# Exchanging the PSUM homes of two kinds of sums, and making weight differences earlier

## The chip, the cores and the metric

The program runs on one core of a Trainium2 chip. The metric is the device time of one execution in microseconds, the median of three runs. A profiled execution gives the trace that is read below.

## The reference

Three layers follow one another. All data are float32.

```
attention   batch 4, heads 8, sequence 576, head dimension 64
  scores = q k^T / 8 + cum[i] - cum[j],  cum = cumsum(log(clip(f, 1e-4, 1)));  causal;  softmax;  times v
  the output is laid out as x: 2304 tokens x 512
first MLP   h = x @ w_in (512 x 1024);  solu = h * softmax(h);  layer norm * g_ln;  @ w_out (1024 x 512)
second MLP  h = max(x @ w2_in (512 x 2048), 0);  out = (h * h) @ w2_out (2048 x 512)
```

## The kernel before

**Order of the work.** All work is entered as steps into a planner (class Plan, line 28). A step has the engines that it may run on with an estimated time on each, the keys that it reads and writes, a priority, and perhaps a slot that it takes from a ring (pp: three one-bank PSUM tiles, hp: two slots, rq: eleven SBUF places for squared products). `lay` puts the steps in an order by these estimates, and the program is emitted in that order. Every engine then works off its own instructions in order. The waits between engines are put in from the tiles that instructions touch, not from the planner's keys. All DMAs are issued from SP's queue, in order.

**PSUM.** Eight banks: `Z` is two tiles of one bank each (z0, z1), `XO` one bank, `HP` (line 325) one tile of two banks, `PP` three tiles of one bank each. In attention z0 and z1 hold scores, XO the sums over v, HP the 1024 products of the first MLP of one token block.

**Precision.** A float32 matmul is three: each operand is split in a high and a low part (`halves`, line 1082: a copy that rounds and a subtraction), and low by high, high by low and high by high are added up in PSUM.

**Second MLP.** It is computed by seven products in place of eight. Hidden columns go in 8 pairs (p = 0 to 7, 256 columns each), tokens in 9 blocks of 256. Block 0 goes through `half_up` (line 1270): 24 matmuls per p into one PSUM bank, then relu and square on ACT. Blocks 1 and 2, 3 and 4, ... go through `unit(b, p)` (line 1300): seven products of six matmuls each in two banks. Products 0 and 1 share the first bank, 2 and 3 the second; they are read (one copy on ACT, three adds on DVE), and products 4, 5 and 6 are added on top of 0, 2 and 3, and read again. Units with odd number take their two banks from ring pp, units with even number take both slots of HP. `half_up` uses pp for p = 0 and 1 and a slot of HP from p = 2 on (HPP).

`step(blk, p)` (line 1376) forms differences of the squared products on DVE, splits them, and adds 21 matmuls to seven down sums of 256 columns each. Sums 0 and 1 lie in z0, 2 and 3 in z1, 4 and 5 in XO, 6 in a pp slot. PE does the group of sums 0, 3, 1 first and then 5, 6, 2, 4. After p = 7 `fold` (line 1435) reads them all: a copy of sum 0 on ACT, then seven adds on DVE in the order 1, 5, 6, 4, 4, 3, 2. The next block starts its sums in the same banks. The last block uses two slots of HP and two of pp.

Units are numbered n = 8 (b - 1) + p. For each unit two steps are due, so PE goes on as unit 0, steps 0 and 1, unit 1, steps 2 and 3, and so on, with steps laid between the products of a unit.

**Weights of the second MLP.** The inputs come as float64 words. Beside attention, `early2` (line 1023) turns them into float32 by integer operations (`convert`, line 668, ending in an add on POOL at line 703) in five staging places (tile free). w2_out (32 pieces of 128 x 256) is stored as it is to the DRAM tensor w2d. Then w2_in follows: per pair seven combinations for `unit` are made (`add2`, line 1056, may run on DVE or POOL), split (`part2`, line 1044) and stored as high and low parts to w2u; the plain halves for `half_up` go to w2d.

In the second MLP `weights2` (line 1133) loads the two w2_out rows of a pair (two loads of 256 KB into two of six staging slots, `load2`, line 1100), makes four differences on DVE in place (`diff`, line 1149, issued at line 1151), and splits the results a (256 columns), b, s and t (512 each) into their places for `step`. `weightsh` (line 1114) does the loading and splitting for `half_up`; `unit` loads its parts from w2u directly.

Of the kernel before, what the change touches and what calls it, by code (L numbers as in the profile page):

```python
# [240 lines left out]
def tile_kernel(ctx: ExitStack, tc: tile.TileContext, q, k, v, f, w_in, w_out, g_ln, w2_in, w2_out, out):  # L241
# [31 lines left out]

    w2d = dram.tile([KF2, 2, P, 512], F32, name="w2d")
    w2u = dram.tile([KF2 // 2, 7, P, 512], F32, name="w2u")
    sb = ctx.enter_context(tc.tile_pool(name="sb", bufs=1))
    ps = ctx.enter_context(tc.tile_pool(name="ps", bufs=1, space=PSUM))
# [50 lines left out]
    NU, NRQ = 13, 11  # L328
    pl = Plan(dict(pp=3, hp=2, rq=NRQ), ("z0", "z1", "xo", "h"))
    uid = [0]  # L330
# [337 lines left out]
    def convert(src, raw, w, hi, lo, n, prio, rawk, wk, outk, gain=None, to=None):  # L668
# [303 lines left out]
    def rk2(ri):  # L972
        return [("2r", ri, z) for z in range(2)]
# [49 lines left out]
    def early2():  # L1023
# [12 lines left out]
        def unit(n, fc, c, hf, prio):  # L1036
            i = n % 5
            convert(
                source2(fc, 2 * c + hf), lambda: both(i), lambda: place(i, 2), None, None, 256,
                prio, ("fr", i), ("fw", i), ("w2d", fc, c, hf), to=w2d[fc, c, :, hf * 256 : hf * 256 + 256],  # L1040
            )
            return i

        def part2(i, p, k, prio):
# [9 lines left out]
            pl.add(dict(dma=1140), lambda: nc.sync.dma_start(w2u[p, k], both(i)), prio, [lk, hk], [("w2u", p, k)])  # L1054

        def add2(i, x, y, op, prio):
# [4 lines left out]
            s = pl.add(dict(dve=335, pool=686), fn, prio, [("fw", x), ("fw", y)], [("fw", i)], port=True)  # L1061

        n = 0
        for fc in range(KF2):
            for hf in range(2):
                unit(n, fc, 1, hf, EARLY0 + n * EARLYP)
                n += 1
        for p in range(KP):
            prio = EARLY1 + p * EARLYQ
            a11, a12, a21, a22 = (unit(n + 2 * a + hf, 2 * p + a, 0, hf, prio + EARLYR * (2 * a + hf)) for a in range(2) for hf in range(2))  # L1070
            n += 4
            prio += 4 * EARLYR
            for i, k in ((a11, 0), (a12, 4), (a22, 5)):
                part2(i, p, k, prio)
            add2(a22, a22, a21, ALU.add, prio)
            add2(a21, a11, a21, ALU.subtract, prio)
            add2(a11, a22, a11, ALU.subtract, prio)
            add2(a12, a12, a11, ALU.subtract, prio)
            for i, k in ((a21, 2), (a22, 3), (a11, 1), (a12, 6)):
                part2(i, p, k, prio)  # L1080

# [17 lines left out]

    def load2(fc, c, prio):  # L1100
        ri = turn[0] % len(RAW)
        turn[0] += 1
        once(("raw", ri), RAW[ri], rk2(ri), prio)
        pl.add(
            dict(dma=1140), lambda: nc.sync.dma_start(RAW[ri][0](), w2d[fc, c]), prio - AHEAD,
            [("w2d", fc, c, z) for z in (0, 1)], rk2(ri),
        )
        return ri
# [5 lines left out]
    def weightsh(p, prio):  # L1114
        for c in range(2):
            ri = load2(2 * p + c, 0, prio)
            for a in "hl":
# [15 lines left out]
    def weights2(p, prio):  # L1133
        W = W2[p]
        rr = [load2(2 * p + i, 1, prio) for i in range(2)]

        def place(nm, n):
# [4 lines left out]
        def split(nm, raw, rk, n):  # L1142
            halves(raw, rk, W[nm + "h"][0], ("w2", p, nm + "h"), W[nm + "l"][0], ("w2", p, nm + "l"), n, prio)

        a, b = slice(0, 256), slice(256, 512)
        r = [[lambda i=i, z=z: RAW[rr[i]][0]()[:, z] for z in (a, b)] for i in range(2)]
        k = [rk2(rr[0]), rk2(rr[1])]

        def diff(dst, x, y, rk, wk):
            def fn():  # L1150
                nc.vector.tensor_tensor(out=dst(), in0=x(), in1=y(), op=ALU.subtract)

            pl.add(dict(dve=335), fn, prio, rk, wk, port=True)

        place("a", 256)
        place("b", 512)
        place("s", 512)
        place("t", 512)
# [65 lines left out]
    m7 = ("pp", "m7")  # L1224
    last8 = [("hp", "l0"), ("hp", "l1"), ("pp", "l2"), ("pp", "l3")]

    def bank(blk, i):
        if blk == NTB - 1:
            return last8[(i + 1) // 2 if i == 6 else i // 2]
        return m7 if i == 6 else ("z0", "z1", "xo")[i // 2]  # L1230

    def psum(k):
        if k[0] == "hp":
            return HP[:, pl.slot[k]]
        if k[0] == "pp":
            return at(k)
        return Z[0] if k == "z0" else Z[1] if k == "z1" else XO.rearrange("p c x -> p (c x)")

# [31 lines left out]
    def half_up(p, prio):  # L1270
        uid[0] += 1
        ck = ("pp" if p < HPP else "hp", uid[0])
        if p == HPP:
            pl.add(dict(dve=0), lambda: None, prio - 5000, [], ["h", "hp"])
        W = H2[p]
        for y, c in ((0, 0), (0, 1), (1, 0), (1, 1)):
            def up(y=y, c=c):
# [10 lines left out]

            rk = [("w2", p, f"u{c}{a}") for a in "hl"] + [("xo", 5 + y, a) for a in range(2)] + ["hp"] * (p >= HPP)
            pl.add(  # L1290
                dict(pe=6 * 116), up, prio, rk, [ck] + ["turn"] * (y + c == 0), take=None if y + c else ck,
                uses=[ck] if y + c else [],
            )
        r = new_r(0, p, prio)
        relu(lambda: psum(ck), lambda: psum(ck), 512, prio, [], [ck], [ck], True)
        square(rof(0, p), lambda: psum(ck), 512, prio, [ck, "rqs"], [r], [ck], True, take=r)

    uprods = [(0, 0), (0, 1), (1, 0), (1, 1), (0, 0), (1, 0), (1, 1)]

    def unit(b, p, prio):  # L1300
        n = (b - 1) * KP + p
        pool = "pp" if n % 2 else "hp"
        uid[0] += 2
        ks = [(pool, uid[0] - 1), (pool, uid[0])]
        lastks[pool] = ks
        s1, s2 = (2 * b - 1, p), (2 * b, p)
# [11 lines left out]
        def prod(i, prio):  # L1318
            m = (7 * n + i) % NU
            sk = ("us", m)  # L1320
            if sk not in first_use:
                once(sk, again(upper[m]), [sk], prio)
            pl.add(
                dict(dma=1140), lambda: nc.sync.dma_start(upper[m][0]().bitcast(F32), w2u[p, i]), prio - UAHEAD,
                [("w2u", p, i)], [sk],
            )

            def fn():
# [12 lines left out]
            pl.add(  # L1341
                dict(pe=6 * 116), fn, prio, [sk, ("xo", i, 0), ("xo", i, 1), "hp"], [k] + ["turn"] * (i == 0),
                take=k if opens_ else None, uses=[] if opens_ else [k],
            )

        def add(dst, x, i, prio, rk, wk, uses=(), take=None):
# [3 lines left out]
            k = ks[uprods[i][0]]  # L1350
            pl.add(dict(dve=344), fn, prio, [k] + rk, wk, uses=[k] + list(uses), take=take)

        for i in range(4):
            prod(i, prio)
        copy(TB, u2f, lambda: half(0), prio, [ks[0]], [uk], [ks[0]])
        add(u2f, u2f, 1, prio, [], [uk])
# [5 lines left out]
        for i in (4, 5, 6):  # L1362
# [3 lines left out]
            dict(act=264), lambda: nc.scalar.activation(out=c11(), in_=half(0), func=AF.Relu), prio, [k, "rqs"], [r1],  # L1366
            uses=[k], take=r1,
        )
# [7 lines left out]
    def step(blk, p, prio):  # L1376
# [329 lines left out]
```

## Time and profile before

| | |
|---|---|
| runs | 863.93, 864.44, 867.23 us, median 864.44 |
| profiled execution | 866.17 us, span of its trace 864.4 us |
| PE busy | 805.0 us (93%) |
| DVE busy | 646.6 us (75%) |
| ACT busy | 543.2 us (63%) |
| POOL busy | 369.8 us (43%) |
| data moved | 151.52 MB, mean 175 GB/s |
| mean granted TensorE clock | 0.984 of 2.4 GHz |

Busy time says how long an engine had something running. Attention and the first MLP fill the first 450 us or so; from about 458 us on PE works on the second MLP. The figures are means over stages that differ, so what a change in one stage is worth has to be read from that stage.

### The profile page before, as it was taken

To read this page: it belongs to the slowest core of one execution; us is meant where nothing else is said; L and a number is where in the kernel's file an instruction comes from. 1 tells how busy PE (TensorE), PEld (TensorE's weight loads), DVE (VectorE), ACT (ScalarE), POOL (GpSimd) and SP (SyncE) were. 2 spreads that over 40 slices of the span, in tenths; PEclk is the share of its full clock that TensorE was granted. 3 is DMA by queue.
4 is the path that set the end of the run, shared out by engine and by line. 5 is a ranking of instruction groups with operands and counts; after the bars stand their busy time and mean duration, and the time that the engine had idled before them with its cause. 6 is when DMAs were issued, how large, how long until landed. Compare 5 with 4: busy or idle time off the path is not lost.

```text
span 864.4 us, 18663 instructions
## 1 busy us (share of the span) xinstructions
PE 805.0 (93%) x6392; PEld 729.0 (84%) x6392; DVE 646.6 (75%) x1655; ACT 543.2 (63%) x1383; POOL 369.8 (43%) x528
## 2 busy tenths in 40 slices
PE   4878899999999999999999888999999999999997
PEld 2556687888888888888989788999999999999997
DVE  8797867887767766866658769888678767876777
ACT  6899977988687887887857555454324433533332
POOL 6468767665587767687753010010111121112110
PEclk9999889999999999999999999999999999999999
DMA  6643336655555555645556666484757676665501
GB/s 208 191 146 116 115 94 205 199 175 171 166 165 177 177 154 167 208 160 166 177 191 205 190 205 243 154 279 144 241 178 237 188 229 205 198 207 172 158 1 49
DMA packets 99869, 151.52 MB, mean 175 GB/s; under 512 B 12128, under 2 KB 41824, under 8 KB 99776
## 3 DMA queue, kind: packets, MB, share of 16 engines
q1 hardware_dynamic: 99776, 150.35, 55.0%
q8 instruction: 50, 0.82, 0.4%
q14 instruction: 43, 0.35, 0.1%
HBM read 117.58 MB, written 32.65 MB: 174 GB/s over the span
## 4 chain that ended last, share of the span: by engine, by line
PE 73%; ACT 11%; DVE 11%; issue 3%; POOL 1%; DVEq 0%; ACTq 0%; POOLq 0%
PE hp L1334 9%; PE pp L1334 9%; PE pp L590 5%; PE z L536 5%; PE xo L610 4%; PE z L1420 3%; PE z L1421 3%; PE pp L777 3%; PE z L1422 3%; PE hp L826 3%; PE pp L779 3%; PE pp L778 3%; ACT adj L571 3%; PE hp L828 3%; PE hp L827 3%
## 5 line engine op out<-in xcount | busy, mean ns | idle before, releaser
L536 PE MATMUL z<-k,q 80*64 80x288 f32 (+17 forms) x384 | 95.8, 348 | 11.9 <-DVE q L501 8.2
L571 ACT ACTIVATE adj<-z,st 64x288 f32<-64x288 f32 (+9 forms) x192 | 95.3, 499 | 17.2 <-DVE st L557 15.2
L590 PE MATMUL pp<-ident,adj 128*128 128x128 f32 (+1 forms) x480 | 82.4, 282 | 16.9 <-ACT adj L571 15.2
L590 PEld LDWEIGHTS pp<-ident,adj 128*128 128x128 f32 (+1 forms) x480 | 52.8, 145 | 43.3 <-ACT adj L571 28.5
L557 DVE CUSTOM_DVE_ANT_0 z<-z,maskb 128x128 f32<-128x128 f32 (+8 forms) x144 | 65.4, 464 | 29.6 <-PE z L536 25.7
L777 PE MATMUL pp<-ln,woh 128*128 128x256 f32 x288 | 84.8, 294 | 2.2 <-DVE ln L906 1.5
L345 ACT COPY pt<-pp 128x256 f32<-128x256 f32 (+5 forms) x167 | 68.1, 418 | 24.3 <-PE pp L590 23.2
L779 PE MATMUL pp<-ln,woh 128*128 128x256 f32 x288 | 81.7, 284 | 0.0
L778 PE MATMUL pp<-ln,wol 128*128 128x256 f32 x288 | 81.7, 284 | 0.0
L1087 DVE TENSOR_TENSOR k<-adj,k 128x512 fp32r<-128x512 f32 x75 | 52.4, 700 | 38.2 <-POOL k L349 26.3
L349 POOL TENSOR_SCALAR k<-adj 128x512 fp32r<-128x512 f32 x39 | 24.2, 620 | 124.2 <-DVE adj L1392 50.7
L536 PEld LDWEIGHTS z<-k,q 128*128 128x128 f32 (+3 forms) x384 | 58.7, 189 | 20.0 <-ACT pt L1526 8.2
L703 POOL TENSOR_TENSOR free<-free 128x256 uint32<-128x256 uint32 x64 | 50.8, 799 | 47.5 <-DVE free L697 42.8
L610 PE MATMUL xo<-pt,vn 128*64 128x128 f32 (+1 forms) x960 | 64.9, 277 | 0.4 <-ACT pt L345 0.3
L826 PE MATMUL hp<-wih,xl 128*128 128x512 f32 x144 | 62.6, 435 | 1.1 <-ACT hp L865 1.1
L349 POOL TENSOR_SCALAR ln<-q 128x384 fp32r<-128x384 f32 x29 | 15.5, 534 | 111.6 <-PE z L1422 42.5
L610 PEld LDWEIGHTS xo<-pt,vn 128*64 128x64 f32 x960 | 51.5, 143 | 11.6 <-issue 6.8
L777 PEld LDWEIGHTS pp<-ln,woh 128*128 128x128 f32 x288 | 55.5, 193 | 4.8 <-DVE ln L906 2.0
L827 PE MATMUL hp<-wil,xh 128*128 128x512 f32 x144 | 57.5, 399 | 0.2 <-DVE wil L707 0.2
L828 PE MATMUL hp<-wih,xh 128*128 128x512 f32 x144 | 57.4, 399 | 0.0
L778 PEld LDWEIGHTS pp<-ln,wol 128*128 128x128 f32 x288 | 55.9, 194 | 0.6
L779 PEld LDWEIGHTS pp<-ln,woh 128*128 128x128 f32 x288 | 55.9, 194 | 0.0
(594 smaller groups left out, 2619.3 us busy)
## 6 DMA issues: line engine op xcount, KB each, us to landing
ln<-w2u SPq DMA_DIRECT2D x119, 256.0 KB
k<-w2u SPq DMA_DIRECT2D x105, 256.0 KB
w2u<-free SPq DMA_DIRECT2D x56, 256.0 KB
kn<-in_k_dram SPq DMA_DIRECT2D x32, 256.0 KB
free<-in_moe_w_out_dram SPq DMA_DIRECT2D x32, 256.0 KB
w2d<-free SPq DMA_DIRECT2D x64, 128.0 KB
free<-in_moe_w_in_dram SPq DMA_DIRECT2D x32, 256.0 KB
vn<-in_v_dram SPq DMA_DIRECT2D x20, 256.0 KB
```

Of the source, the lines that this page charges most:

```text
L345: nc.scalar.copy(dst(), src())
L536: nc.tensor.matmul(dst, lhsT=ql[0:r, p, 0:m], rhs=rhs, start=(g == 0), stop=(g == 1))
L571: nc.scalar.activation(out=adj[0:m, c[1] : c[2]], in_=Z[c[0]][0:m, 0 : c[2] - c[1]], func=AF.Exp, bias=st[0:m, low : low + 1], scale=-1.0, ...
L590: nc.tensor.transpose(at(sk)[:, (c - g) * m : (c - g + 1) * m], adj[0:m, zc : zc + P], ident[0:m, 0:m])
L610: nc.tensor.matmul(XO[own[j], g // 2, off : off + m], lhsT=VN[vslot[b, c]][:, (g + j) * D : (g + j + 1) * D], rhs=PT[(s - h + g + j) % NPT ...
L777: nc.tensor.matmul(px, lhsT=woh[:, fc, w], rhs=lo, start=(fc == 0), stop=False)
L778: nc.tensor.matmul(px, lhsT=wol[:, fc, w], rhs=hi, start=False, stop=False)
L779: nc.tensor.matmul(px, lhsT=woh[:, fc, w], rhs=hi, start=False, stop=(fc == KF - 1))
L826: nc.tensor.matmul(HP[:, c], lhsT=XL[i][:, cc, :], rhs=wih[:, cc, w], start=(cc == 0), stop=False)
L827: nc.tensor.matmul(HP[:, c], lhsT=XH[i][:, cc, :], rhs=wil[:, cc, w], start=False, stop=False)
L828: nc.tensor.matmul(HP[:, c], lhsT=XH[i][:, cc, :], rhs=wih[:, cc, w], start=False, stop=(cc == KC - 1))
L1334: nc.tensor.matmul(half(i), lhsT=l, rhs=r[:, x], start=(i in (0, 2) and c + k == 0), stop=(c + k == 3), skip_group_check=True,)
```

## The change

The two kinds of sums exchange homes. Units with an even number and all of `half_up` use z0 and z1; down sums 0 to 3 use the two banks of HP (keys h0 and h1). The last block's sums 0 to 3 use z0 and z1 in place of HP.

The differences of w2_out are made in `early2`, beside attention, with `add2`. For pairs 0 to 6 the seven pieces of 128 x 256 (a, b in two, s in two, t in two) are stored as float32 to w2f, and `weights2` loads them in four loads and splits them. For the last pair (NPRE = 1) the pieces are split in `early2` as well and stored to w2s, and `weights2` loads high and low parts straight into their places, in eight loads. The planner's estimate of such loads goes from 1140 to 900 ns per 256 KB (LOAD2).

```diff
-    w2d = dram.tile([KF2, 2, P, 512], F32, name="w2d")
+    w2d = dram.tile([KF2, P, 512], F32, name="w2d")
+    w2f = dram.tile([KF2 // 2 - NPRE, 7, P, 256], F32, name="w2f")
+    w2s = dram.tile([NPRE, 7, P, 512], F32, name="w2s")
...
-    more("k10", 5, 1, upper)
+    upper += carve("k10", [512] * 5)
...
+        def keep(i, p, k, prio):
+            if p >= KP - NPRE:
+                part2(i, w2s[p + NPRE - KP, k], ("w2s", p, k), prio)
+            else:
+                pl.add(dict(dma=570), lambda: nc.sync.dma_start(w2f[p, k], place(i, 2)), prio, [("fw", i)], [("w2f", p, k)])
...
-        for fc in range(KF2):
-            for hf in range(2):
-                unit(n, fc, 1, hf, EARLY0 + n * EARLYP)
-                n += 1
+        for p in range(KP):
+            prio = EARLY0 + 4 * p * EARLYP
+            r00, r01, r10, r11 = (
+                unit(n + 2 * a + hf, 2 * p + a, 1, hf, prio + EARLYP * (2 * a + hf)) for a in range(2) for hf in range(2)
+            )
+            n += 4
+            prio += 4 * EARLYP
+            for i, k in ((r00, 0), (r10, 1), (r11, 2)):
+                keep(i, p, k, prio)
+            add2(r00, r01, r00, ALU.subtract, prio)
+            add2(r01, r11, r01, ALU.subtract, prio)
+            for i, k in ((r00, 3), (r01, 4)):
+                keep(i, p, k, prio)
+            add2(r11, r11, r00, ALU.subtract, prio)
+            add2(r10, r11, r10, ALU.subtract, prio)
+            for i, k in ((r10, 5), (r11, 6)):
+                keep(i, p, k, prio)
...
     def weights2(p, prio):
-        rr = [load2(2 * p + i, 1, prio) for i in range(2)]
-        split("a", r[0][0], k[0][0:1], 256)
-        diff(r[0][0], r[0][1], r[0][0], k[0][1:], k[0][0:1])
-        split("b", RAW[rr[1]][0], k[1], 512)
-        diff(r[0][1], r[1][1], r[0][1], k[1][1:], k[0][1:])
-        split("s", RAW[rr[0]][0], k[0], 512)
-        diff(r[1][1], r[1][1], r[0][0], k[0][0:1], k[1][1:])
-        diff(r[1][0], r[1][1], r[1][0], k[1][1:], k[1][0:1])
-        split("t", RAW[rr[1]][0], k[1], 512)
+        for nm, n in (("a", 256), ("b", 512), ("s", 512), ("t", 512)):
+            if p < KP - NPRE:
+                src = w2f[p, c[0]] if n == 256 else w2f[p, c[0] : c[0] + 2].rearrange("c p x -> p c x")
+                ri = load2(src, [("w2f", p, k) for k in c], n, prio)
...
+                continue
+            for y, a in enumerate("hl"):
+                def fn(dst=W[nm + a][0], c=c, n=n, y=y):
+                    src = w2s[p + NPRE - KP, c[0] : c[0] + n // 256, :, y * 256 : y * 256 + 256]
...
-    last8 = [("hp", "l0"), ("hp", "l1"), ("pp", "l2"), ("pp", "l3")]
+    last8 = ["z0", "z1", ("pp", "l2"), ("pp", "l3")]
-        return m7 if i == 6 else ("z0", "z1", "xo")[i // 2]
+        return m7 if i == 6 else ("h0", "h1", "xo")[i // 2]
...
     def half_up(p, prio):
-        ck = ("pp" if p < HPP else "hp", uid[0])
+        ck = f"z{p % 2}"
...
     def unit(b, p, prio):
-        pool = "pp" if n % 2 else "hp"
-        ks = [(pool, uid[0] - 1), (pool, uid[0])]
+        ks = [("pp", uid[0] - 1), ("pp", uid[0])] if n % 2 else ["z0", "z1"]
...
-HPP = 2
+NPRE, LOAD2 = 1, 900
```

## Rows read from the trace of the kernel before

**Rows 1.** The page: the chain that ended last, shares by engine.

```profile
PE 73%; ACT 11%; DVE 11%; issue 3%; POOL 1%; DVEq 0%; ACTq 0%; POOLq 0%
```

**Rows 2.** What PE waited for, 458 to 845 us: total, times, longest (us).

```profile
PE hp L1334 <- DVE xw L1348: 3.5, 4, 1.0
PE hp L1334 <- ACT xw L345: 3.2, 6, 0.9
PE hp L1334 <- ACT q L1366: 3.2, 6, 0.7
PE hp L1284 <- ACT q L1253: 2.2, 3, 0.7
PE hp L1284 <- ACT hp L1248: 2.2, 3, 0.8
PE hp L1334 <- issue: 1.5, 1, 1.5
PE hp L1334 <- ACT adj L1366: 0.9, 2, 0.5
PE hp L1334 <- ACT xh L1366: 0.9, 2, 0.5
PE z L1420 <- DVE ln L1087: 0.6, 1, 0.6
PE hp L1334 <- ACT qn L1366: 0.5, 1, 0.5
PE hp L1284 <- ACT adj L1253: 0.4, 1, 0.4
```

**Rows 3.** Timeline of PE: start, us, engine, line, operation, [idle before <-releaser].

```profile
616.55 0.87 PE L1334 MATMUL pp<-woh,ln 128*128 128x256 f32 x6
...
626.44 0.87 PE L1334 MATMUL hp<-woh,ln 128*128 128x256 f32 x6
627.15 1.57 PE L1334 MATMUL hp<-wol,ln 128*128 128x256 f32 x12
629.18 0.97 PE L1334 MATMUL hp<-wol,ln 128*128 128x256 f32 x6 [0.46 <-ACT xw L345]
...
699.37 0.87 PE L1334 MATMUL pp<-woh,k 128*128 128x256 f32 x6
```

**Rows 4.** Timeline of ACT: the copies of product 0 in both homes.

```profile
618.16 0.37 ACT L345 COPY maskb<-pp 128x256 f32<-128x256 f32 x1 [1.10 <-PE pp L1334]
...
628.76 0.37 ACT L345 COPY xw<-hp 128x256 f32<-128x256 f32 x1 [1.76 <-PE hp L1334]
```

**Rows 5.** Stretches: busy us (instructions) by engine, PE clock, DMA share, GB/s.

```profile
150.00:250.00 100.00, 96.19 (x767) 83.73 (x766) 79.39 (x212) 81.14 (x230) 63.80 (x90) 0.98 0.59 178
250.00:400.00 150.00, 148.02 (x1214) 126.98 (x1213) 105.10 (x282) 123.05 (x346) 110.24 (x159) 1.00 0.52 169
495.00:505.00 10.00, 7.61 (x46) 6.87 (x44) 3.73 (x7) 3.75 (x7) 0.83 (x2) 0.83 0.49 161
515.00:520.00 5.00, 5.00 (x45) 5.00 (x44) 4.91 (x13) 2.52 (x6) 0.00 (x0) 1.00 1.01 324
```

**Rows 6.** Timeline at one block end: PE, ACT and DVE, one after the other.

```profile
595.55 0.28 PE L1422 MATMUL z<-pt,k 128*128 128x256 f32 x1
...
600.26 0.28 PE L1420 MATMUL z<-free,ln 128*128 128x256 f32 x1
...
596.33 0.35 ACT L345 COPY x<-z 128x256 f32<-128x256 f32 x1
...
599.48 0.74 DVE L1437 TENSOR_TENSOR kn<-x,z 128x256 f32<-128x256 f32 x2
```

**Rows 7.** Line 1151, two of 8 groups: ns min/median/max, first to last start.

```profile
L1151 DVE TENSOR_TENSOR kn<-kn x8: 419/426/717, 464.7 to 528.3; 128x256 f32<-128x256 f32 x8
...
L1151 DVE TENSOR_TENSOR adj<-adj x2: 417/420/424, 478.3 to 520.3; 128x256 f32<-128x256 f32 x2
```

**Rows 8.** Line 1059, the subtractions and adds of add2, in the same columns.

```profile
L1059 POOL TENSOR_TENSOR free<-free x32: 723/738/1159, 251.0 to 438.1; 128x256 f32<-128x256 f32 x32
```

More of the change, by code (lines that the diff above doesn't have):

```diff
@@ L328, in tile_kernel @@
     NU, NRQ = 13, 11
-    pl = Plan(dict(pp=3, hp=2, rq=NRQ), ("z0", "z1", "xo", "h"))
+    pl = Plan(dict(pp=3, hp=2, rq=NRQ), ("z0", "z1", "xo", "h", "h0", "h1"))
     uid = [0]
@@ L714, in convert @@
         pl.add(dict(pool=tt), a5, prio, [lk], [wk])
+        if to is False:
+            return
         if to is not None:
@@ L1039, in unit, with part2 @@
                 source2(fc, 2 * c + hf), lambda: both(i), lambda: place(i, 2), None, None, 256,
-                prio, ("fr", i), ("fw", i), ("w2d", fc, c, hf), to=w2d[fc, c, :, hf * 256 : hf * 256 + 256],
+                prio, ("fr", i), ("fw", i), ("w2d", fc, hf), to=False if c else w2d[fc, :, hf * 256 : hf * 256 + 256],
             )
             return i
-        def part2(i, p, k, prio):
+        def part2(i, dst, key, prio):
             hi, lo = (lambda: place(i, 0).bitcast(F32R)), (lambda: place(i, 1).bitcast(F32R))
@@ L1053, in part2 @@
             s = pl.add(dict(dve=335, pool=686), sub, prio, [w, lk], [hk], port=True)
-            pl.add(dict(dma=1140), lambda: nc.sync.dma_start(w2u[p, k], both(i)), prio, [lk, hk], [("w2u", p, k)])
+            pl.add(dict(dma=1140), lambda: nc.sync.dma_start(dst, both(i)), prio, [lk, hk], [key])
         def add2(i, x, y, op, prio):
@@ L1073, in early2 @@
             for i, k in ((a11, 0), (a12, 4), (a22, 5)):
-                part2(i, p, k, prio)
+                part2(i, w2u[p, k], ("w2u", p, k), prio)
             add2(a22, a22, a21, ALU.add, prio)
@@ L1079, in early2 @@
             for i, k in ((a21, 2), (a22, 3), (a11, 1), (a12, 6)):
-                part2(i, p, k, prio)
+                part2(i, w2u[p, k], ("w2u", p, k), prio)
     def halves(raw, rk, hi, hk, lo, lk, n, prio, uses=()):
@@ L1098, in tile_kernel, with load2 @@
     turn = [0]
-    def load2(fc, c, prio):
+    def load2(src, rk, n, prio):
         ri = turn[0] % len(RAW)
@@ L1103, in load2, with fn @@
         once(("raw", ri), RAW[ri], rk2(ri), prio)
[L1104 to L1107, printed above, removed]
+        def fn():
+            dst = RAW[ri][0]()[:, 0:n]
+            nc.sync.dma_start(dst.rearrange("p (c x) -> p c x", x=256) if len(src.shape) == 3 else dst, src)
+        pl.add(dict(dma=LOAD2 * n / 512), fn, prio - AHEAD, rk, rk2(ri)[0 : n // 256])
         return ri
@@ L1115, in weightsh @@
         for c in range(2):
-            ri = load2(2 * p + c, 0, prio)
+            ri = load2(w2d[2 * p + c], [("w2d", 2 * p + c, z) for z in range(2)], 512, prio)
             for a in "hl":
@@ L1134, in weights2 @@
         W = W2[p]
-        rr = [load2(2 * p + i, 1, prio) for i in range(2)]
-        def place(nm, n):
+        o = 0
+        for nm, n in (("a", 256), ("b", 512), ("s", 512), ("t", 512)):
+            c = range(o, o + n // 256)
+            o += n // 256
             for a in "hl":
@@ L1140, in place @@
                 claim(W[nm + a], [("w2", p, nm + a)], prio)
[L1142 to L1158, printed above, removed]
-        split("a", r[0][0], k[0][0:1], 256)
-        diff(r[0][0], r[0][1], r[0][0], k[0][1:], k[0][0:1])
-        split("b", RAW[rr[1]][0], k[1], 512)
-        diff(r[0][1], r[1][1], r[0][1], k[1][1:], k[0][1:])
-        split("s", RAW[rr[0]][0], k[0], 512)
-        diff(r[1][1], r[1][1], r[0][0], k[0][0:1], k[1][1:])
-        diff(r[1][0], r[1][1], r[1][0], k[1][1:], k[1][0:1])
-        split("t", RAW[rr[1]][0], k[1], 512)
+            if p < KP - NPRE:
+                src = w2f[p, c[0]] if n == 256 else w2f[p, c[0] : c[0] + 2].rearrange("c p x -> p c x")
+                ri = load2(src, [("w2f", p, k) for k in c], n, prio)
+                halves(
+                    lambda ri=ri, n=n: RAW[ri][0]()[:, 0:n], rk2(ri)[0 : n // 256], W[nm + "h"][0], ("w2", p, nm + "h"),
+                    W[nm + "l"][0], ("w2", p, nm + "l"), n, prio,
+                )
+                continue
+            for y, a in enumerate("hl"):
+                def fn(dst=W[nm + a][0], c=c, n=n, y=y):
+                    src = w2s[p + NPRE - KP, c[0] : c[0] + n // 256, :, y * 256 : y * 256 + 256]
+                    nc.sync.dma_start(
+                        dst().bitcast(F32).rearrange("p (c x) -> p c x", x=256), src.rearrange("c p x -> p c x")
+                    )
+                pl.add(
+                    dict(dma=LOAD2 * n / 512), fn, prio - AHEAD, [("w2s", p, k) for k in c], [("w2", p, nm + a)]
+                )
     def xload(ri, g, tok, prio):
@@ L1229, in bank @@
             return last8[(i + 1) // 2 if i == 6 else i // 2]
-        return m7 if i == 6 else ("z0", "z1", "xo")[i // 2]
+        return m7 if i == 6 else ("h0", "h1", "xo")[i // 2]
     def psum(k):
[L1233 to L1237, printed above, removed]
+        if k in ("h0", "h1"):
+            return HP[:, int(k[1])]
+        if k in ("z0", "z1"):
+            return Z[int(k[1])]
+        return XO.rearrange("p c x -> p (c x)") if k == "xo" else at(k)
     def acc(blk, i):
@@ L1270, in half_up @@
     def half_up(p, prio):
-        uid[0] += 1
-        ck = ("pp" if p < HPP else "hp", uid[0])
-        if p == HPP:
-            pl.add(dict(dve=0), lambda: None, prio - 5000, [], ["h", "hp"])
+        ck = f"z{p % 2}"
         W = H2[p]
@@ L1287, in up @@
                         )
[L1289 to L1293, printed above, removed]
+            rk = [("w2", p, f"u{c}{a}") for a in "hl"] + [("xo", 5 + y, a) for a in range(2)]
+            pl.add(dict(pe=6 * 116), up, prio, rk, [ck] + ["turn"] * (y + c == 0))
         r = new_r(0, p, prio)
-        relu(lambda: psum(ck), lambda: psum(ck), 512, prio, [], [ck], [ck], True)
-        square(rof(0, p), lambda: psum(ck), 512, prio, [ck, "rqs"], [r], [ck], True, take=r)
+        relu(lambda: psum(ck), lambda: psum(ck), 512, prio, [], [ck], [], True)
+        square(rof(0, p), lambda: psum(ck), 512, prio, [ck, "rqs"], [r], [], True, take=r)
     uprods = [(0, 0), (0, 1), (1, 0), (1, 1), (0, 0), (1, 0), (1, 1)]
@@ L1301, in unit @@
         n = (b - 1) * KP + p
-        pool = "pp" if n % 2 else "hp"
         uid[0] += 2
-        ks = [(pool, uid[0] - 1), (pool, uid[0])]
-        lastks[pool] = ks
+        ks = [("pp", uid[0] - 1), ("pp", uid[0])] if n % 2 else ["z0", "z1"]
+        lastks[n % 2] = ks
         s1, s2 = (2 * b - 1, p), (2 * b, p)
@@ L1323, in prod @@
             pl.add(
-                dict(dma=1140), lambda: nc.sync.dma_start(upper[m][0]().bitcast(F32), w2u[p, i]), prio - UAHEAD,
+                dict(dma=LOAD2), lambda: nc.sync.dma_start(upper[m][0]().bitcast(F32), w2u[p, i]), prio - UAHEAD,
                 [("w2u", p, i)], [sk],
@@ L1341, in prod @@
             pl.add(
-                dict(pe=6 * 116), fn, prio, [sk, ("xo", i, 0), ("xo", i, 1), "hp"], [k] + ["turn"] * (i == 0),
-                take=k if opens_ else None, uses=[] if opens_ else [k],
+                dict(pe=6 * 116), fn, prio, [sk, ("xo", i, 0), ("xo", i, 1)], [k] + ["turn"] * (i == 0),
+                take=k if opens_ and n % 2 else None, uses=slots_of([] if opens_ else [k]),
             )
@@ L1350, in add @@
             k = ks[uprods[i][0]]
-            pl.add(dict(dve=344), fn, prio, [k] + rk, wk, uses=[k] + list(uses), take=take)
+            pl.add(dict(dve=344), fn, prio, [k] + rk, wk, uses=slots_of([k]) + list(uses), take=take)
         for i in range(4):
             prod(i, prio)
-        copy(TB, u2f, lambda: half(0), prio, [ks[0]], [uk], [ks[0]])
+        copy(TB, u2f, lambda: half(0), prio, [ks[0]], [uk], slots_of([ks[0]]))
         add(u2f, u2f, 1, prio, [], [uk])
@@ L1366, in unit @@
             dict(act=264), lambda: nc.scalar.activation(out=c11(), in_=half(0), func=AF.Relu), prio, [k, "rqs"], [r1],
-            uses=[k], take=r1,
+            uses=slots_of([k]), take=r1,
         )
@@ L1408, in step @@
         if p == 0 and blk in (0, NTB - 1):
-            for k in [m7] if blk == 0 else last8:
-                pl.add(dict(pe=0), lambda: None, prio + DOWN, lastks[k[0]] if blk else [], [k], take=k)
+            for k in [m7] if blk == 0 else last8[2:]:
+                pl.add(dict(pe=0), lambda: None, prio + DOWN, lastks[1] if blk else [], [k], take=k)
+            if blk == 0:
+                pl.add(dict(pe=0), lambda: None, prio, [], ["h", "h0", "h1"])
         end = blk == NTB - 1 and p == KP - 1
```

## The prediction

> **What bounds the kernel now.** I read the page first, its chain of waits above all: the chain that ended last is 73% PE, with ACT and DVE at 11% each [rows 1]. So the time is what PE has to do plus what makes it stop, and the change takes no matmul away: all it can win is stops of PE. The second view is therefore the list of what PE waited for between 458 and 845 us, which is the second MLP [rows 2]. The reader is to see one thing there: every wait of an up product (L1334) and of a half-block product (L1284) is of tile hp; no line names an up product in pp. Yet units alternate between hp and pp, and run the same code.
>
> Third, the timeline of one unit in each home [rows 3, 4]. In hp, PE issues product 0 (6 matmuls), products 1 and 2 (12), and product 3 starts late, at 629.18, "<-ACT xw L345". That ACT instruction is the copy of product 0's half. Product 0 lies in bank 0 of hp, product 3 in bank 1, so no datum passes between them. The wait runs the other way too: matmuls come every (627.15 - 626.44) / 6 = 0.118 us, so product 1 is issued by 626.44 + 12 x 0.118 = 627.86, but the copy starts at 628.76, after product 2 (bank 1), due at 628.57. In pp, where the two banks are two tiles, product 1 is issued by 616.55 + 12 x 0.118 = 617.97 and the copy starts at 618.16, and PE goes on. So the order is kept for the two-bank tile as a whole.
>
> Fourth, busy time by stretch [rows 5], for what lies beside the changed steps.
>
> **What one stop costs.** Product 3 of the hp unit was due at 627.15 + 12 x 0.118 = 628.57; it came 0.61 later, and its six matmuls took 0.97 in place of 0.87 [rows 3]. That is 0.71, where the view shows 0.46 idle: 0.25 is to be added to each idle time.
>
> **Part 1: up products into one-bank tiles.**
> - Units: the six hp L1334 lines with a named releaser add up to 12.2 us in 21 stops [rows 2]; with 21 x 0.25 = 5.3, 17.5 us. A cross-check: one block of 8 units and 16 steps, from pp unit to pp unit, takes 699.37 - 616.55 = 82.82 us [rows 3], and its 8 x 42 + 16 x 21 = 672 matmuls 79.3; 3.5 are stops, against 17.5 / 4 = 4.4 in the mean block.
> - Half-block products: three L1284 lines, 4.8 us in 7 stops [rows 2], 1.8 on top: 6.6 us. Here PE writes slot B while ACT squares slot A.
> - Clock: between 495 and 505 us, right after those stops, the granted clock is 0.83 of 2.4 GHz, so for about a third of that stretch it was at 1.2 [rows 5]. PE was busy 7.61 us: 0.17 x 7.61 = 1.3 us, which I let go with the stops.
>
> I take all of this as gone: z0 and z1 are then what pp is now. What is late next are true dependencies: product 4 adds onto product 0's place, and must wait for its copy; pp has the same and shows no wait.
>
> **Part 2: down sums into hp.** They are written 72 times and read only at the 8 block ends before the last (block 8 uses z0, z1 and two pp slots). There the first read, ACT's copy of sum 0, now follows the first group of three sums. If hp is one tile, it must follow sum 2, third of the second group: 9 matmuls x 0.118 = 1.06 us later. Seven adds on DVE follow it, and the next block's first group waits for the last: at one such end the copy is at 596.33, the last reads end at 599.48 + 0.74 = 600.22, and PE writes z at 600.26 [rows 6]. So there is no slack after the chain, and up to 8 x 1.06 = 8.5 us can come on. But the copy at 596.33 already starts after the last matmul of sum 2, issued at 595.55, since ACT was behind; it would lose nothing. Behind that copy on ACT stand the next unit's copies and relus, for which PE waits. Bounds 0 and 8.5; I take 1.
>
> **Part 3: differences moved beside attention.** Out of the second MLP go 32 subtractions on DVE of 0.42 us (8 rows, the first and the last in [rows 7]), 13 us, and for the last pair four copies and four subtractions more. Worth to PE: the stops where DVE was late, "issue" 1.5 and z L1420 0.6 [rows 2], with 2 x 0.25: 2.6. I count all of it. The rest of DVE's relief is hidden under PE.
> Beside attention come 32 subtractions, and for the last pair 7 copies and 7 subtractions: 46 operations. Such subtractions run now in the second half of attention, 32 of 32 on POOL at 0.738 us [rows 8]; 46 x 0.738 = 33.9 us, the upper bound if nothing covered them. The lower bound is a gain of all of PE's idle time in 150-250, 3.8 us, by another order. Cover: POOL is busy 64% there, DVE 79% [rows 5]. And 250-400, which carries this same kind of work, has less idle PE (2.0 us in 150) than 150-250 has (3.8 in 100). I take 1.5, near the lower end for that reason.
> By the Trainium skill (page "SBUF — State Buffer", section "SBUF: two separate sides") a GpSimd instruction and a DVE instruction with two SBUF inputs, or in a two-port mode, lock one another out for a whole instruction. It speaks against this part: by it the 33.9 us would hold DVE too. The row of such subtractions, at most 1159 ns against a median of 738, lets one believe in some lock; the idle PE of 250-400 says it is covered.
>
> **Part 4: loads.** Per pair two loads become four, and rows of 1 KB instead of 2. Before: 16 x 262,144 bytes = 4.2 MB. After: 7 x 917,504 + 1,835,008 (the last pair, high and low parts straight into place) = 8.3 MB. The stores beside attention double likewise. The 4.1 MB more fall between about 440 and 540 us, where the most seen is 324 GB/s at a DMA share of 1.01 (515-520) [rows 5]: 12.6 us if nothing covers them, nothing if all is covered. SP issues in order: a load that waits for one of the six staging slots holds up the loads of up weights (w2u) behind it, and PE waits for those. The planner is also told 900 instead of 1140 ns per load, so it packs them closer. I take 4 us, which also stands for PE, now earlier, meeting true waits (the split blocks of x) after the half-block stage: at mean share 0.49 (495-505) most is covered, at 515-520 not.
> At nothing: the small piece taken out of the pool (one of 17; 16 are used), the last block's sums in z0 and z1 (the same reads in the same order).
>
> **Sum.** Won: 17.5 + 6.6 + 1.3 + 2.6 = 28.0. Given back: 1 + 1.5 + 4 = 6.5. Profiled execution 866.17 us (span 864.4 and 1.77 around it): 844.7. The median of the runs, 864.44, is 1.73 lower, which would make it 842.9; I say 844, with 840 to 849 as the forecast's own range.
>
> **Rivals.**
> 1. Loads bind the start of the second MLP: 12.6 in place of 4, 853. For: 324 GB/s is already reached. Against: PE never waits for a DMA in [rows 2]. Chance 0.13.
> 2. The whole-tile order bites at block ends: 8.5 in place of 1, 852. For: no slack at 600.26. Against: ACT is behind anyway. 0.09.
> 3. Nothing given back: 866.17 - 28.0 = 838. For: pp units show not one stop. 0.08.
> 4. The stops are not of the two-bank tile but of the order of work, and z units stop as hp units did. Then only DVE's 2.6 is won and 5.5 given back: 869, within 0.5%. Against: pp has the same order. 0.05.
> 5. Slower: the 46 operations, in order on POOL with attention's own (or holding DVE), end up on attention's chain, 33.9 at most: 844.7 - 1.5 + 33.9 = 877. It decides from 23 us on, two thirds of them uncovered. Against: POOL has 1% of the chain [rows 1]. 0.04.
>
> **How the numbers follow.** The forecast has 0.61. With rivals 1 to 3, faster by over 0.5% (4.3 us, about what can be told from no change) has 0.91; rival 4 is "same", 0.05; rival 5 "slower", 0.04. The range takes in rival 3 and rivals 1 and 2 with 4 us for both partly at once: 837 to 857.
>
> **What would show it.** Right: no PE wait of L1334 in z or pp; no L1284 wait on ACT; granted clock 1.0 around 495; copies of product 0 some 0.2 us after product 1 in both homes; PE's idle time from 458 to 845 under 7 us. Part 2 shows as waits of PE at L1420 to L1422 on hp for DVE; part 3 as more idle PE in 150-250 and a second MLP that starts later than 458; part 4 as PE or PEld waits for DMA, or a DMA share near 1 around 500. I am wrong if hp's stops reappear under z.

## The result, and the profile after

The changed kernel takes 841.41 us (median of 4 runs, 840.30 to 842.40), the kernel before 864.18 in the same comparison (861.42 to 867.23): a ratio of 0.9735, 95% interval 0.970 to 0.977. The forecast was 844 with 837 to 857. The profiled execution took 840.3 us (span 838.5), where the sum gave 844.7: the mechanism was right, and 4.4 us of the sum were not.

The page after, engines and the chain that ended last (for [rows 1]):

```profile
PE 793.9 (95%) x6392; PEld 723.5 (86%) x6392; DVE 633.1 (75%) x1614; ACT 550.3 (66%) x1415; POOL 392.4 (47%) x543
PE 70%; ACT 10%; DVE 8%; DMA 5%; POOL 4%; issue 3%; SPq 0%; DVEq 0%; POOLq 0%; ACTq 0%
```

DMA is new on the chain with 5%, and POOL has 4% where it had 1%. What PE waited for in the second MLP, 458 to 820 us (line, releaser: total, times, longest); the unit's products are now L1345, its adds L1359, `half_up` is L1299, the down products L1433 to L1435, the splitting subtraction on DVE L1110:

```profile
PE xo L1433 <- DVE k L1110: 2.1, 2, 1.6
PE pp L1345 <- DMA ln<-w2u: 1.1, 1, 1.1
PE pp L1433 <- DVE k L1110: 0.7, 1, 0.7
PE z L1345 <- DVE q L1359: 0.3, 1, 0.3
PE z L1345 <- DVE wol L1110: 0.2, 1, 0.2
```

All 28 stops of hp in [rows 2] are gone; no up product waits for ACT in either home. What is left is late data: splits and one add on DVE, and one load. One unit in z, timeline of PE (for the hp unit of [rows 3]):

```profile
550.54 0.87 PE L1345 MATMUL z<-woh,k 128*128 128x256 f32 x6
551.25 1.57 PE L1345 MATMUL z<-wol,k 128*128 128x256 f32 x12
552.66 0.87 PE L1345 MATMUL z<-wol,ln 128*128 128x256 f32 x6
```

and on ACT the copy of its product 0 (for [rows 4]):

```profile
552.16 0.37 ACT L347 COPY xw<-z 128x256 f32<-128x256 f32 x1 [1.05 <-PE z L1345]
```

Product 1 is issued by 550.54 + 12 x 0.118 = 551.96, the copy starts 0.20 later, and product 3 comes right behind product 2: what pp showed before.

Stretches of before that [rows 5] do not have, and then the stretches of after (columns as in [rows 5]):

```profile
450.00:550.00 100.00, 89.74 (x702) 85.42 (x700) 78.73 (x175) 55.87 (x115) 14.03 (x19) 0.98 0.66 210
500.00:525.00 25.00, 22.30 (x177) 21.48 (x176) 18.68 (x45) 13.25 (x28) 2.26 (x4) 0.97 0.71 234
550.00:800.00 250.00, 241.52 (x2016) 238.55 (x2016) 187.51 (x492) 99.06 (x201) 37.68 (x65) 1.00 0.63 203
```

```profile
150.00:250.00 100.00, 96.88 (x776) 83.24 (x775) 78.19 (x212) 85.77 (x242) 70.73 (x93) 1.00 0.62 183
250.00:400.00 150.00, 148.44 (x1221) 126.85 (x1220) 104.98 (x280) 130.02 (x366) 114.52 (x158) 1.00 0.57 183
450.00:550.00 100.00, 96.30 (x798) 95.26 (x797) 77.67 (x172) 59.64 (x128) 20.79 (x28) 0.98 0.90 290
495.00:505.00 10.00, 8.92 (x76) 8.72 (x75) 8.90 (x18) 7.61 (x18) 1.58 (x2) 1.00 0.91 268
500.00:525.00 25.00, 21.87 (x169) 21.26 (x168) 22.46 (x54) 14.37 (x29) 2.92 (x4) 0.93 1.02 340
550.00:800.00 250.00, 250.00 (x2123) 250.00 (x2123) 195.21 (x509) 100.32 (x204) 43.23 (x74) 1.00 0.64 205
```

From 550 to 800 PE does not stop at all. One stretch got worse: in 500 to 525 PE is busy 21.87 us where it was 22.30, with the DMA share at 1.02 (the view adds up the times of the packets that start in a stretch, so a share can exceed 1). The clock of 450 to 550 is 0.98 in both: its fall at 495 to 505 is gone, and there is another in 505 to 510 (last section).

To compare traces I use a measure that a stop, a slow matmul and a low clock all enter. The work that is left at a time is PE's remaining matmuls, by 0.1177 us for 256 columns (the 0.118 of above, unrounded; and 0.228 and 0.085 for the few of 512 and the transposes); what the clock takes beyond it is lost. In us:

| | span | work left at 450 | lost 450 to 550 | lost after 550 |
|---|---|---|---|---|
| before | 864.4 | 378.5 | 16.1 | 19.8 |
| after | 838.5 | 375.5 | 6.7 | 6.3 |

Some 4.5 of the last column is the tail behind the last matmul, in every kernel. So of the span's 25.9 us, 22.9 were lost after 450 before and no longer are, nearly all in the second MLP, and 3.0 are PE being ahead at 450.

### The profile page after: what moved, and what is told of

It reads as the page before. It is cut to its first block, busy times and chain, and to the rows that moved or that the text cites. A ratio compares the mean times of both kernels' runs of the same rounds, so it can differ in the third digit from the quotient of the medians.

```text
span 838.5 us, 18711 instructions
## 1 busy us (share of the span) xinstructions
PE 793.9 (95%) x6392; PEld 723.5 (86%) x6392; DVE 633.1 (75%) x1614; ACT 550.3 (66%) x1415; POOL 392.4 (47%) x543
## 4 chain that ended last, share of the span: by engine, by line
PE 70%; ACT 10%; DVE 8%; DMA 5%; POOL 4%; issue 3%; SPq 0%; DVEq 0%; POOLq 0%; ACTq 0%
PE pp L1345 9%; PE z L1345 9%; PE pp L592 5%; PE xo L612 5%; PE z L538 5%; PE hp L1433 3%; PE hp L1435 3%; PE hp L1434 3%; PE hp L830 3%; PE hp L832 3%; PE pp L781 3%; PE hp L831 3%; PE pp L783 3%; PE pp L782 3%; ACT adj L573 2%
## 5 line engine op out<-in xcount | busy, mean ns | idle before, releaser
L538 PE MATMUL z<-k,q 80*64 80x288 f32 (+17 forms) x384 | 93.4, 344 | 9.0 <-DVE q L503 8.2
L592 PE MATMUL pp<-ident,adj 128*128 128x128 f32 (+1 forms) x480 | 81.3, 280 | 17.1 <-ACT adj L573 16.1
L1110 DVE TENSOR_TENSOR k<-adj,k 128x512 fp32r<-128x512 f32 x75 | 53.0, 706 | 38.6 <-POOL k L351 27.7
L351 POOL TENSOR_SCALAR ln<-q 128x384 fp32r<-128x384 f32 x30 | 16.1, 535 | 112.4 <-PE hp L1435 46.7
```

The lines of the kernel that those rows point to most:

```text
L538: nc.tensor.matmul(dst, lhsT=ql[0:r, p, 0:m], rhs=rhs, start=(g == 0), stop=(g == 1))
L592: nc.tensor.transpose(at(sk)[:, (c - g) * m : (c - g + 1) * m], adj[0:m, zc : zc + P], ident[0:m, 0:m])
```

## The experiments

The theory: the exchange of homes makes the whole gain, since a two-bank tile's order is kept as a whole; the early differences cost a little and win little. The rivals: the differences win a part of their own; the order of work makes the stops; loads are what binds now. All ratios are to the kernel before on the same chip. The new estimate of 900 ns per load (LOAD2) was not tried by itself.

**e1 and e6: the homes alone.** Differences, loads and their estimates stay as before.

```diff
-        ck = ("pp" if p < HPP else "hp", uid[0])
+        ck = f"z{p % 2}"
...
-        ks = [(pool, uid[0] - 1), (pool, uid[0])]
+        ks = [("pp", uid[0] - 1), ("pp", uid[0])] if n % 2 else ["z0", "z1"]
...
-        return m7 if i == 6 else ("z0", "z1", "xo")[i // 2]
+        return m7 if i == 6 else ("h0", "h1", "xo")[i // 2]
```

> Only the PSUM homes are exchanged; the differences of w2_out stay in the second MLP. Theory (the stops come from the two-bank tile): all stops of L1334 and L1284 named in the trace of before go, and attention is untouched, so 864.2 - 28.0 + 2.6 (DVE late, stays) + 2 to 4 (DVE, now pressed by a PE that is ahead, late more often between 500 and 550) = 841 to 845 us; the homes alone carry at least four fifths of the 22.8 us. Rival (the homes only help because the early differences freed DVE): about 13 us from 550 us on and nothing before, 851 us, with PE waits for DVE between 500 and 550 grown to 8 us or more.

> Only the homes exchanged, as in the first experiment, in more rounds: 839 to 842 us and within 1.5 us of the changed kernel if the early differences add nothing; 843 or more if they do.

Measured: 840.31 us (837.61 to 842.7), ratio 0.973 [0.969, 0.977]; again, with five rounds, 840.46 (837.88 to 841.88), 0.973 [0.970, 0.975]. That is the whole gain, and e1 lies a little below the 841 to 845 that was expected. Lost after 450: 10.3 and 10.8 us in place of 35.9, so 25 to 26 us come from the exchange. PE's waits of e1 between 430 and 860 us (L1327 is the unit, L1415 the down products, L1087 the split; the first and third are of the stages before):

```profile
PE pp L590 <- ACT xc L345: 1.8, 1, 1.8
PE z L1327 <- DVE adj L1341: 1.4, 1, 1.4
PE pp L903 <- POOL e L887: 0.8, 1, 0.8
PE pp L1415 <- DVE k L1087: 0.7, 1, 0.7
PE hp L1415 <- DVE ln L1087: 0.6, 1, 0.6
PE xo L1415 <- DVE k L1087: 0.2, 1, 0.2
```

No stop of PE for ACT is left in the second MLP. What there is, is DVE, which is busy 24.38 of 25 us between 500 and 525, where the early differences leave it 22.46:

```profile
500.00:525.00 25.00, 23.43 (x196) 22.97 (x195) 24.38 (x59) 16.61 (x35) 1.43 (x2) 1.00 0.85 288
```

**e2: the early differences alone.** The homes stay as before; `early2`, `load2`, `weights2` and LOAD2 are those of the change.

```diff
+            add2(r00, r01, r00, ALU.subtract, prio)
...
+                src = w2f[p, c[0]] if n == 256 else w2f[p, c[0] : c[0] + 2].rearrange("c p x -> p c x")
```

> Only the differences are made early (with the loads and the 900 ns of the planner); the PSUM homes are those of before. Theory: the 28 stops of PE on tile hp stay; what is won is the 2.6 us in which DVE was late and the 3 us by which attention was over earlier in the changed kernel: 859 to 863 us. Rival (the early differences carry half of the gain): 853 us or less.

Measured: 862.37 us (858.36 to 864.62), 0.997 [0.995, 1.000]. The stops of hp are there again, 26 with a named releaser where before had 28, the first lines of PE's waits being (L1302 is `half_up`, L1352 the unit):

```profile
PE hp L1302 <- ACT hp L1266: 3.1, 4, 1.0
PE hp L1352 <- DVE xw L1366: 2.9, 3, 1.0
PE hp L1352 <- ACT xw L347: 2.8, 6, 0.5
```

Alone, the second part of the change wins 0.3%, and the interval ends at 0.9997: that can hardly be told from no change. Work left at 450 is 375.1, 3.4 less than before.

**e3: stops back, order kept.** The changed kernel, but z0 and z1 are the halves of one two-bank tile. The planner knows keys, not tiles, so the order that it writes is that of the changed kernel: in the two traces the instructions of PE, ACT, DVE and POOL follow one another in the same order.

```diff
-    Z = [ps.tile([P, 512], F32, name=f"z{i}") for i in range(2)]
+    ZT = ps.tile([P, 2, 512], F32, name="zt")
+    Z = [ZT[:, i] for i in range(2)]
```

> The changed kernel with z0 and z1 as the two halves of one two-bank tile, as hp is; planned order, homes and early differences as in the changed kernel. Theory (waits are kept per tile): in the second MLP products 3 and 6 of the units in z wait for ACT and DVE again, some 21 stops and 12 us of idle PE after 490 us of work, half-block products too (7 stops, 5 us), where the changed kernel has 0.5 us; attention, whose heads alternate between z0 and z1, gets slower as well, by 20 to 80 us, so the total tells nothing. Rival (the order of work made the stops): no PE wait of an up product in z beyond the 0.5 us.

Measured: 910.26 us in a single run. The waits of PE, 458 to 900 us (L1300 is `half_up`, L1346 the unit):

```profile
PE zt L1300 <- ACT zt L1267: 4.9, 6, 1.2
PE zt L1346 <- ACT q L1378: 3.9, 6, 1.4
PE zt L1300 <- ACT q L1272: 3.0, 4, 0.7
PE zt L1346 <- ACT xw L348: 2.8, 6, 0.5
```

The stops reappear under the new name, with the order of work unchanged: this settles that they belong to the tile. 46.7 us are lost after 450, 33.7 more than in the changed kernel. The rest of the span's 70 is ahead of 450 (work left then is 411.8, 36.3 more): attention's scores lie in z too ("PE zt L539 <- ACT adj L574: 7.9, 18, 0.8" between 100 and 450 us), and stop in the same way. So e3 shows the mechanism, and not the size of it for the change.

**e4: the last pair as the others.** NPRE 1 becomes 0: the last pair's pieces are stored as float32 and split in the second MLP, 0.9 MB less to load.

```diff
-NPRE, LOAD2 = 1, 900
+NPRE, LOAD2 = 0, 900
```

> The changed kernel with NPRE = 0: the last pair is loaded as float32 and split in the second MLP like the others, 0.92 MB less to load around 520 us and as much less to store, but four copies and four subtractions (2.4 us of DVE) more. Theory (between 500 and 530 us DMA bandwidth binds, 340 to 387 GB/s at a share of 1.02 to 1.10): 0.92 MB / 350 GB/s = 2.6 us less, 838.5 to 841 us. Rival (DVE binds there): 1 to 3 us more, 842.5 to 845 us.

Measured: 840.77 us (839.7 to 842.18), 0.974 [0.971, 0.978]: not told from the change. The loss between 450 and 550 is 5.7 in place of 6.7, where 2.6 less was expected; a load is still late there ("PE pp L1345 <- DMA ln<-w2u: 1.5, 1, 1.5").

**e5: the change once more,** on the chip of e6 to e8 and with five rounds, for the comparison with the homes alone.

> The changed kernel once more, beside the homes alone on the same chip and in more rounds. Theory (the early differences give 2 to 4 us in attention and take as much back in loads after it): both within 1.5 us of each other, 839 to 842. Rival (they are worth what they take from DVE): this one 2.5 us or more under the homes alone.

Measured: 839.55 us (838.23 to 840.25), 0.972 [0.969, 0.974], against 840.46 for e6: 0.9 us apart, with ranges that overlap. What the early differences add to the homes cannot be told. One half-block product waits for ACT here ("PE z L1299 <- ACT q L1271", 0.4 us), which the first execution of the change does not have. Two effects lie under it: work left at 450 is 373.2 against 378.0 of e6, and the loss between 450 and 550 is 8.0 against 4.8.

**e7: half of the moved loads.** The changed kernel, but only the first half of each 256 KB load of differences is moved (2.75 MB less).

```diff
+            if len(src.shape) == 3:
+                nc.sync.dma_start(dst[:, 0:256], src[:, 0])
+                return
```

> The changed kernel, of each 256 KB load from w2f only the first half is moved (the other half of the staging slot keeps what it held; the output is not the reference's): 21 x 131,072 = 2.75 MB less, same order, same work on all engines. Theory (loads bind PE between 500 and 525 us): DMA share there under 0.95, PE's 3.1 us of idle time and the fall of the clock to 0.93 go, 2 to 5 us less, 836.5 to 839.5. Rival (DVE, not the loads, is late there): the same stops at L1433 for DVE, within 1 us of the changed kernel.

Measured: 835.62 us (834.1 to 836.52), 0.967 [0.965, 0.970], 3.9 less than e5. The loss between 450 and 550 is 3.6 in place of 6.7 and 8.0. Its waits no longer name a DMA:

```profile
PE xo L1436 <- DVE k L1110: 2.2, 2, 1.6
PE pp L1436 <- DVE k L1110: 0.7, 1, 0.7
PE z L1348 <- DVE q L1362: 0.3, 1, 0.3
```

The load's stop and the fall of the clock are gone (500 to 525 has 1.00, after had 0.93 and e5 0.86); the 1.6 us stop for the split k is not, so it is not a matter of these bytes. Nor did the DMA share there fall under 0.95, as was expected: it is 0.98, and PE's idle time in 500 to 525 went from 3.1 to 2.2 us only. The time lies below the 836.5 to 839.5 expected. So the bytes left out had cost 3 to 4 us in the start of the second MLP, through one late load and the clock behind it.

**e8, e9 and e10: a balance.** If all differences early make DMA late, and none make DVE late, some early should do both less. Pairs in EARLYSET get their differences beside attention, the others as in the kernel before; NPRE is 0.

```diff
+            if p not in EARLYSET:
+                for i, fc, hf in ((r00, 0, 0), (r01, 0, 1), (r10, 1, 0), (r11, 1, 1)):
...
+                continue
...
+        if p not in EARLYSET:
...
+EARLYSET = (0, 1, 2, 4, 6)
```

> The changed kernel with the early differences for pairs 0, 1, 2, 4 and 6 alone (no pair split early); pairs 3, 5 and 7 load two rows of 512 and form their differences on DVE as before: 2.1 MB less to load around 510 to 540 us, 12 differences (5 us of DVE) more. Theory (loads and DVE both near their limit there, so that sharing helps): 837.5 to 840 us, best of all. Rival (either limit costs the same): 840 to 842.

> Early differences for five pairs once more, for a second profile: 834 to 837 us. Theory (its gain over the changed kernel is fewer bytes after attention and less idle PE in attention by its order): PE idle between 150 and 400 us again 2 to 3 us, against 4 to 5 in the changed kernel, whatever the granted clock of the first 150 us. Rival (its first profile merely had a better clock): idle 4 us or more, and 838 us or more.

> Early differences for pairs 0, 1 and 2 alone, whose loads fall before 500 us, where the DMA share of the homes alone is 0.65 to 0.76; pairs 3 to 7 as before. Theory (loads bind only after 500 us): PE's loss between 450 and 550 us at most that of five pairs, 835 to 838 us. Rival (DVE then binds between 500 and 550, as in the homes alone): 838 to 841.

Measured, five pairs early (0, 1, 2, 4, 6): 835.0 us (834.0 to 837.47), 0.967 [0.965, 0.970]; on another chip 837.11 (834.99 to 839.25), 0.968 [0.965, 0.971]. Three pairs early (0, 1, 2): 836.1 (834.06 to 837.27), 0.966 [0.963, 0.970]. On the chip of e5 the five-pair kernel is below the change by 4.5 us without overlap of the ranges; five and three are not told apart. The gain of five pairs was underestimated (837.5 to 840 expected for e8). For e9 the theory had asked for 2 to 3 us of PE's idle time between 150 and 400, the rival for 4 or more; it is 3.5, which decides nothing. The stretches of e10:

```profile
450.00:550.00 100.00, 99.88 (x836) 98.85 (x835) 84.68 (x196) 61.06 (x127) 20.47 (x27) 1.00 0.80 259
500.00:525.00 25.00, 25.00 (x215) 25.00 (x214) 24.43 (x61) 15.39 (x32) 2.52 (x4) 1.00 0.90 307
```

In this execution PE has no gap between 500 and 525, and loses 0.6 us of the 100, less than the homes alone; five pairs lose 4.7 and 5.7 there, about as much as the homes alone. So the price of the change's second part is real and can be taken off. Against e5, the span of e8 is 5.1 us shorter, 3.3 of it won here; that of e10 is 1.8 shorter, with 7.4 won here and 5.5 given back ahead of 450. That three pairs are faster than the change is read from ratios alone (0.966 against 0.972 and 0.9735), since the change did not run on that chip.

## Why the prediction was right, and where it was not

**One stop's cost and part 1: right.** 17.5 + 6.6 + 1.3 = 25.4 us were to go; the homes alone took 25 to 26 away. The 0.25 us beside each idle time was needed: the listed idle time of the 28 stops is 17.0 us [rows 2]. The clock of 495 to 505 went with the stops as said, 0.83 [rows 5] to 1.00, and in the homes alone it is 1.00 over 450 to 550. In the changed kernel other stops bring a fall of the same size 10 us later, which belongs to part 4.

**Part 2: mis-sized, 1 us for 0.** That the order of the whole tile is kept shows at one of the eight block ends, the last, where ACT has nothing else to do and the copy of sum 0 waits for sum 2 (L1435 is its last line):

```profile
812.73 0.37 ACT L347 COPY x<-hp 128x256 f32<-128x256 f32 x1 [0.54 <-PE hp L1435]
```

At the other seven ACT is busy up to the copy, as the prediction read it from [rows 6], so the order delays nothing there; at three of these PE does other products between the two groups, and the copy comes ahead of sum 2. One block end after, on PE, ACT, DVE and PE:

```profile
619.37 0.28 PE L1435 MATMUL hp<-pt,k 128*128 128x256 f32 x1
...
619.68 0.37 ACT L347 COPY x<-hp 128x256 f32<-128x256 f32 x1
...
622.98 0.75 DVE L1450 TENSOR_TENSOR kn<-x,hp 128x256 f32<-128x256 f32 x2
...
624.08 0.28 PE L1433 MATMUL hp<-free,ln 128*128 128x256 f32 x1
```

PE writes hp 0.35 us after the last read ended (622.98 + 0.75), without a stop, and no wait for hp stands in its list: it has the next unit's products to do in z or pp meanwhile. The touch of two times in [rows 6] that I read as "no slack" was an order of work that fits, not a chain.

**Part 3: the step that failed.** "I take 1.5" for the work beside attention; measured is a gain of 3.0, which is the whole miss of 4.4 us (-3.0 against +1.5). POOL did get 22.6 us more to do, and all 64 operations of `add2` ran there (L1063):

```profile
L1063 POOL TENSOR_TENSOR free<-free x64: 722/736/1192, 127.2 to 461.3; 128x256 f32<-128x256 f32 x64
```

PE's idle time between 150 and 400 went from 3.8 + 2.0 [rows 5] to 3.1 + 1.6 us. The lower end of the range, "another order", named this possibility, and I put the term on the other side of zero. The lock between GpSimd and DVE that the Trainium skill states (page "SBUF — State Buffer", section "SBUF: two separate sides") may show in the longest of the subtractions, 1192 ns against a median of 736; no loss of PE between 150 and 400 goes with twice as many of them: its idle time there is 4.1 to 6.0 us in after, e2, e4, e5 and e7, and 5.8 to 6.3 in before, e1 and e6.

The start of the second MLP does not tell it. `half_up`'s first product is earlier in after than in before (ns min/median/max, first to last start; before, then after):

```profile
L1284 PE MATMUL pp<-vn,k x36: 276/276/278, 458.2 to 462.9; 128*128 128x256 f32 x36
```

```profile
L1299 PE MATMUL z<-vn,k x96: 274/282/362, 454.9 to 483.8; 128*128 128x256 f32 x96
```

But in e6, without the early differences, it starts at 454.9 too, with as much work left at 450 as before. How much of the 3.0 is the change is only partly settled. e2 (375.1), e4 (376.4), e7 (374.4), e5 (373.2) and the five-pair kernels (371.1, 373.4) all have less work left at 450 than before (378.5) and the homes alone (380.6, 378.0); the three-pair one (378.7) has not. Why all or five pairs early put PE ahead, and three do not, stays open (PE's idle time between 150 and 400 is 2.4 and 3.5 us with five, 6.5 with three); single executions differ by some us on their own (last section).

The other 2.6 us of this part, DVE's lateness, did not go in sum: I had put 2.1 us of PE's waits down to it [rows 2], after has 3.3. The largest of them, 1.5, seems to go: the homes alone have a like one of 1.4 ("PE z L1327 <- DVE adj L1341"), after one of 0.3. In its place comes a new stop of 1.57 at L1433. PE is 3 us ahead at 450 and some 12 at 550, and meets DVE's work sooner. In the homes alone every named wait of the second MLP is for DVE.

**Part 4: right in size.** 4 us, measured 2 to 4: the loss of 450 to 550 of after and e5 lies 1.9 to 3.7 above that of e1 and e6, and e7 gives 3 to 4 back. The 324 GB/s behind the upper bound were misread: before itself has 335 between 520 and 525 (last section). Two stops of PE make most of it (timeline of after):

```profile
504.39 0.97 PE L1345 MATMUL pp<-wol,ln 128*128 128x256 f32 x6 [1.08 <-DMA ln<-w2u]
506.94 0.38 PE L1433 MATMUL xo<-woh,k 128*128 128x256 f32 x1 [1.57 <-DVE k L1110]
```

The first is a late load. The second is the order on DVE: the split of k stands behind two adds (505.40 and 505.86, on pp) that wait for the products PE makes after the first stop. It is there in e7 as well, without the first.

**The sum.** From 450 on 28.0 - 1 - 4 = 23.0 was forecast and 22.9 measured. That closeness is in part luck: the 2.6 of DVE, which came back as other waits for it, stands against folds that cost nothing and against loads a little cheaper.

**The rivals.** 1 (loads bind) is out by its size: PE does wait for a load, but the price is the 2 to 4 us of the forecast's own term and not 12.6. 2 is out: the order is kept, and costs nothing. 3 (838.2 for the profiled execution) lies nearer to its 840.3 than the sum's 844.7 does, but for another reason than it gave: something was given back, and something won. 4 is out by e3. 5 is out: the POOL operations are covered.

**The signs.** No wait of an up product on ACT, clock 1.0 at 495, the copy 0.2 us behind product 1, and for part 4 a wait for a load and a DMA share near 1 around 500: as listed. PE's idle time in the second MLP was to be under 7 us: it is 4.4 between 458 and 820, ahead of the last block's end. The signs that did not come are those of part 2, waits for hp at block ends, and of part 3, more idle PE in 150 to 250 and a later start of the second MLP.

## What to carry to other kernels

When PE waits for an engine that works in another bank than the one PE wants, compare the same code in another home: if one home stops and the other does not, the waits belong to the tile, and one tile per bank took them away here. The two-bank tile cost nothing where it is written 72 times and read at 8 block ends. After stops are gone, look at what the engine meets earlier: here work moved out of DVE came back as loads, and moving three to five of eight pairs won some 4 us more than moving all.

## What was not expected of the hardware

DMA moved more than the 324 GB/s that the prediction took as its most [rows 5]. In the changed kernel:

```profile
515.00:520.00 5.00, 5.00 (x45) 5.00 (x44) 4.14 (x13) 1.55 (x4) 0.00 (x0) 1.00 1.10 355
520.00:525.00 5.00, 4.52 (x39) 4.31 (x38) 4.44 (x14) 2.27 (x4) 0.00 (x0) 1.00 1.05 387
```

The halved rows are not what brings this. In the first of these stretches 1604 of 1722 packets are under 2 KB, in the second 117 of 1061, and it is the second that moves more. The kernel before, with rows of 2 KB, reaches as much in stretches that the prediction left out, and the homes alone have 400 GB/s between 515 and 520:

```profile
520.00:525.00 5.00, 4.54 (x39) 4.33 (x38) 3.95 (x11) 2.77 (x7) 0.62 (x1) 1.00 0.95 335
605.00:610.00 5.00, 5.00 (x45) 5.00 (x44) 3.35 (x10) 2.21 (x5) 1.13 (x2) 1.00 1.04 392
```

Even 387 GB/s would make 10.6 us of 4.1 MB. That they cost 2 to 4 means that most of them are covered: the DMA share over 450 to 550 is 0.71 in the homes alone (227 GB/s) and 0.90 in the changed kernel (290).

The granted clock falls with the two stops above, of 1.08 and 1.57 us within 4 us:

```profile
505.00:510.00 5.00, 3.43 (x21) 3.22 (x20) 4.84 (x12) 2.01 (x4) 0.00 (x0) 0.78 1.02 336
```

So PE ran at 1.2 GHz in place of 2.4 for a part of these 5 us. In e7 the second stop is there alone (1.57 us, ending at 503.60), in e1 one of 1.42 (ending at 522.04), and the clock of 500 to 525 is 1.00 in both. The pair of stops stands in e5 (1.20 and 1.71) and e4 (1.55 and 1.68) too, and the clock falls in both (0.86 and 0.93 in 500 to 525); in e8 and e9, where two stops of 1.3 to 1.7 lie further apart, it stays at 1.00. A late load right before a late split thus cost more than the sum of the two waits: by the rows of 500 to 525 some 1.5 us more in after (0.07 of 21.87) and 3 in e5 (0.14 of 21.61), an estimate.

The clock of the first 150 us differs between executions of one order: between 100 and 150 us it is 0.86 in after and 0.93 in e5, which is the same kernel. Over 0 to 150 it is 0.91 in after, and 0.93 in e5 and in before: of the 150 us the missing share is 13.5 us in after and 10.5 in the other two, an upper bound of what PE lost by it, as PE is not always busy there. So two single profiles differ by some us that are of no kernel's making, and the work left at 450 has to be read with that in mind.
